# Float64 weights to float32: a two-byte shift of the load, one copy and one shift-and-OR in place of five operations

## Chip, cores and metric

The kernel runs on one core of one Trainium2 chip. The metric is device microseconds of one execution. A NeuronCore has TensorE (PE; its weight loads are listed as PEld), VectorE (DVE), ScalarE (ACT), GpSimd (POOL) and SyncE (SP), which here issues nearly all DMAs, in program order. Sixteen DMA engines serve the core.

## The reference

Three layers follow each other. Four batches with eight heads of causal attention over 576 tokens (head size 64) with a decay term, then a feed-forward layer with a leaky ReLU over 2304 tokens, then a second layer with a SoLU, a layer norm and an output product:

```python
scores = scale * q @ k.T + (cum[:, None] - cum[None, :])   # causal, softmax
x = softmax(scores) @ v                                    # (2304, 512)
h = x @ w_in                                               # w_in (512, 2048), float64
x = np.maximum(0.01 * h, h) @ w_out                        # w_out (2048, 512), float64
h = x @ w_in2                                              # (512, 1024), float64
solu = h * softmax(h)
out = ((solu - mean) / sqrt(var + 1e-6) * g_ln) @ w_out2   # (1024, 512), float64
```

The four weight matrices arrive as float64. [...]

## The kernel before

**Weights.** The weights are cut into 48 chunks of 128 x 512 values (512 KB each as float64): 16 of `w_in` (tiles `wi`, `wib`), 16 of `w_out` (`wo`, `wob`), 8 each of the second layer's matrices (again in `wi` and `wo`). Function `weight` handles a chunk. A DMA brings it into a staging tile (`wst`, three of them, for 17 chunks; later `raw` or `raw2`, two of them, which attention's `kq` loads and layer 2 use as well). ACT writes the absolute value of the upper words into one of two work tiles `wk` (L793). DVE clamps it (L794), shifts it by three bits and masks it (L795), puts the sign bit in (L797) and the upper bits of the lower words (L799). From `wk` a copy to the first half of the weight tile follows (L425 on ACT, L428 on DVE, L432 on POOL), rounded to the format that TensorE takes, and a subtraction (L440, or L436 with a scale) writes the rest to the second half. The staging tile is free after L799, the work tile after the subtraction.

**Order.** A planner (`Plan.run`) goes through all operations before the program is written. Each has a duration by a formula, a priority and the buffers that it needs; the planner hands each engine its next operation, and picks the engine where several are allowed (`flex`, `copy_f`, `sub_f`). What it decides is a fixed program order for each engine; at run time each instruction waits for its inputs in that order.

**Stages.** Sixteen pairs of heads (`pair`) go through attention: score products into `ps_s`, the row maximum (L692, L711), the exponential (L642), a high and a low float16 part of the probabilities `hl` (L425, L436), a transposing DMA `pt<-hl` (L468), and products with V into `ps_v`. Batch 0 (four pairs) is handled together with the first 18 weight chunks. When all `wst` tiles and other early tiles are done with, `main` puts the `x` and `g` tiles in their place, and the first feed-forward blocks (`ffn_a`, nine blocks of 256 tokens, with the first nine `wi` and `wo` chunks) run interleaved with the attention of batches 1 to 3; the block that begins inside batch 1 needs all four pairs of that batch. Then the other 30 chunks are turned, and `ffn_b` and `layer2` follow to the end.

Of the kernel before, what the change touches and what calls it, by code (L numbers as in the profile page):

```python
# [8 lines left out]
F32R = mybir.dt.float32r  # L9
F16 = mybir.dt.float16  # L10
I32 = mybir.dt.int32
BF16 = mybir.dt.bfloat16
AF = mybir.ActivationFunctionType
ALU = mybir.AluOpType
# [50 lines left out]
NEG = -8.0e9  # L65
LNS = 1024.0

F64_LO = 2.0 ** -15
F64_HI = 122876.0
PS = 2.0 ** -15  # L70


# [256 lines left out]
def dve(n):  # L329
    return 1.042 * n + 70  # L330


def dve2(n):
    return 0.521 * n + 70
# [22 lines left out]
def body(tc, kqa, kq, vt, f, one, wa, w2i, w2o, gln, out):  # L357
# [44 lines left out]

    early = ExitStack()
    ep = early.enter_context(tc.tile_pool(name="early", bufs=1, side="right"))
    P.tag("wst", tiles(ep, "wst", NWST, [128, 1024], I32))
    qa = ep.tile([128, 2, KD, 512], F32, name="qa")
    P.tag("qa", [qa])
    P.tag("qb", tiles(ep, "qb", NQB, [128, 2, KB], F32))
# [65 lines left out]
    def setup():  # L474
        nc.gpsimd.memset(qa[64:66, 0], 1.0)
        nc.vector.memset(qa[64:66, 1], 1.0)
        nc.vector.memset(mask, 0.0)
        one_at = P.tags["sd"].free[-1][:, 0:128]
        nc.vector.memset(one_at, 0.0)
        nc.gpsimd.affine_select(  # L480
            one_at, one_at, pattern=[[-1, 128]], compare_op=ALU.not_equal, fill=1.0, base=0, channel_multiplier=1)
        nc.vector.tensor_copy(ident, one_at)
        nc.vector.memset(mask4, 0.0)
        nc.gpsimd.affine_select(
            mask[:, 384:512], mask[:, 384:512], pattern=[[-1, 128]], compare_op=ALU.is_ge,
            fill=NEG, base=0, channel_multiplier=1)
        for o in (0, 64):
            nc.gpsimd.affine_select(
                mask4[o:o + 64, 512:576], mask4[o:o + 64, 512:576], pattern=[[-1, 64]],
                compare_op=ALU.is_ge, fill=NEG, base=0, channel_multiplier=1)  # L490
        nc.gpsimd.memset(halfm, -0.5)
        nc.vector.memset(zcol, 0.0)

    def row(h, p):
# [292 lines left out]

    def weight(src, dst, prio, scale=None, lead=None):
        s, k = P.buf(stage[0]), P.buf("wk")
        load(s, lambda: s.t[:, 0:1024].bitcast(I32), lambda: src.bitcast(I32), 524288, prio - LDW if lead is None else lead)  # L790
        word = lambda j: s.t[:, 0:1024].bitcast(I32).rearrange("p (n t) -> p n t", t=2)[:, :, j]
        kf = lambda: k.t.bitcast(F32)
        P.op(ACT, act(512), lambda: nc.scalar.activation(kf(), word(1).bitcast(F32), AF.Abs), prio, w=[k], r=[s])  # L793
        P.op(DVE, dve2(512), lambda: nc.vector.tensor_scalar(kf(), kf(), F64_LO, F64_HI, op0=ALU.max, op1=ALU.min), prio, rw=[k])  # L794
        P.op(DVE, dve2(512), lambda: nc.vector.tensor_scalar(  # L795
            k.t, k.t, 3, 0x3FFFFFF8, op0=ALU.logical_shift_left, op1=ALU.bitwise_and), prio, rw=[k])
        P.op(DVE, dve(512), lambda: nc.vector.scalar_tensor_tensor(  # L797
            k.t, word(1), -0x40000000, k.t, op0=ALU.bitwise_and, op1=ALU.bitwise_or), prio, rw=[k], r=[s])
        P.op(DVE, dve(512), lambda: nc.vector.scalar_tensor_tensor(  # L799
            k.t, word(0), 29, k.t, op0=ALU.logical_shift_right, op1=ALU.bitwise_or), prio, rw=[k], r=[s])  # L800
        copy_f(lambda: dst.t[:, 0], kf, 512, prio, scale=scale, w=[(dst, 0)], r=[k])
        sub_f(lambda: dst.t[:, 1], kf, lambda: dst.t[:, 0].bitcast(F32), 512, prio, scale=scale, w=[(dst, 1)],
              r=[k, (dst, 0)])

    WI, WO, W2I, W2O = {}, {}, {}, {}
    stage = ["wst"]
# [18 lines left out]
    def hidden(c, xb, n, pst, gt, prio, eprio):  # L825
# [11 lines left out]

        P.op(PE, 12 * mmr(n), pe, prio, w=[ps, (g, "slot")], r=xb + [w])
        h = lambda: ps.t[:, 0:n]
        P.op(ACT, act(n, 0, True), lambda: nc.scalar.activation(g.t[:, 0, 0:n], h(), AF.Prelu, alpha=0.01), eprio, w=[(g, 0)], r=[ps])  # L840
        P.op(ACT, act(n, 0, True), lambda: nc.scalar.activation(h(), h(), AF.Prelu, alpha=0.01), eprio, rw=[ps])  # L841
        P.op(DVE, dve(n) + 60, lambda: nc.vector.tensor_tensor(  # L842
            g.t[:, 1, 0:n], h(), g.t[:, 0, 0:n].bitcast(F32), op=ALU.subtract), eprio, w=[(g, 1)], r=[ps, (g, 0)])
        return g
# [31 lines left out]
    def ffn_a(blk, prio):  # L876
# [4 lines left out]
        for d in range(KD):  # L881
            ps, yo = P.buf("ps_f"), P.buf("yo")
            for q in range(2):
                cs = range(FA // 2 * q, FA if q else FA // 2)

                def pe(cs=cs, d=d, ps=ps):
                    for c in cs:
# [1 line left out]

                P.op(PE, 3 * len(cs) * mmr(TB), pe, prio + EPD + d, r=[gs[c] for c in cs] + [WO[c] for c in cs],  # L890
                     **({"w": [ps]} if q == 0 else {"rw": [ps]}))
            copy_f(lambda yo=yo: yo.t, lambda ps=ps: ps.t[:, 0:TB], TB, eprio + EPD + d, engs=(ACT, DVE), psum=True, w=[yo], r=[ps])
            YPD[blk].append(move(lambda d=d: yp_d[blk][:, d], lambda yo=yo: yo.t, 128 * TB * 4, prio - 3000, r=[yo]))

    def ffn_b(tb, prio):
# [19 lines left out]
        for d in range(KD):  # L915
            y32, y = P.buf("yo"), P.buf("y2")
            yw = yps[d // 2]
            P.op(DVE, dve(TB), lambda d=d, y32=y32, yw=yw: nc.vector.tensor_tensor(
                y32.t, at[d](), yw.t[:, d % 2], op=ALU.add), eprio + 20, w=[y32], r=[py[d], yw])
            copy_f(lambda y=y: y.t[:, 0], lambda y32=y32: y32.t, TB, eprio + 20, w=[(y, 0)], r=[y32])  # L920
            sub_f(lambda y=y: y.t[:, 1], lambda y32=y32: y32.t, lambda y=y: y.t[:, 0].bitcast(F32), TB, eprio + 20,
                  w=[(y, 1)], r=[y32, (y, 0)])
# [66 lines left out]
    def layer2_out(tt, ln, oprio, eprio, deps=()):  # L989
# [8 lines left out]
                mm(po.t, ll, wh, False, c == NC2 - 1)  # L998

        P.op(PE, 24 * mmr(512), pe2, oprio, w=[po], r=list(ln.values()) + list(W2O.values()), deps=deps)  # L1000
        P.op(ACT, act(512, 0, True), lambda: nc.scalar.activation(ot.t, po.t, CP, scale=1.0 / LNS), eprio, w=[ot], r=[po])
        move(lambda: out[128 * tt:128 * tt + 128, :], lambda: ot.t, 262144, -4000, r=[ot])

    def flat(l):
# [125 lines left out]
```

## Time and profile before

| | |
|---|---|
| median of 3 runs | 875.1 us (873.83 to 875.33) |
| profiled execution | 875.05 us, span 873.3 us |
| PE busy | 791.8 us, 91% of the span |
| DVE busy | 581.2 us, 67% |
| ACT busy | 477.8 us, 55% |
| POOL busy | 343.1 us, 39% |
| mean granted clock of TensorE | 0.986 of full speed |

The shares of busy time are means over stages that differ: attention with the first weights (to about 118 us), attention with feed-forward blocks (to about 380 us), the other weights (to about 520 us), and feed-forward and layer 2 alone.

### The profile page before, as it was taken

Reading aid. Unit: us, or ns where it says so; the run is one execution under the profiler, and the core shown is the slowest. Engines: PE = TensorE matmul, PEld = TensorE weight load, DVE = VectorE, ACT = ScalarE, POOL = GpSimd, SP = SyncE. Lnnn points to the kernel's source line nnn. Section 1 sums busy time; section 2 is a strip of 40 time slices with the busy share of each in tenths; the row PEclk is TensorE's granted clock in tenths of the full one; section 3 lists DMA queues with packets and bytes.
Section 4 is the critical chain, followed back from the end, with each engine's and each line's share of the span. In section 5 each row is a group of like instructions: output and inputs, shape, how many; then the busy total and the mean of one; then the engine's idle time right before and its main releaser. Section 6 shows DMA issues by size and latency. Waiting matters only on the chain.

```text
span 873.3 us, 15789 instructions
## 1 busy us (share of the span) xinstructions
PE 791.8 (91%) x5648; PEld 706.2 (81%) x5648; DVE 581.2 (67%) x1405; ACT 477.8 (55%) x1221; POOL 343.1 (39%) x394
## 2 busy tenths in 40 slices
PE   2647799996799999999999999999999999999997
PEld 2323379995689998999999988899988888988985
DVE  6799987888887888858868985424542345234551
ACT  3765778896888988765535543323423243323421
POOL 4465376654674564026212325221422232213321
PEclk9999999998699999999999999999999999999999
DMA  7899589978998895946544423321413041313113
GB/s 217 181 243 232 137 184 191 211 190 184 216 176 202 168 233 134 216 109 187 182 145 134 137 93 85 61 50 48 109 37 69 29 109 38 84 10 77 25 37 96
DMA packets 181960, 114.97 MB, mean 132 GB/s; under 512 B 147030, under 2 KB 163054, under 8 KB 181850
## 3 DMA queue, kind: packets, MB, share of 16 engines
q1 hardware_dynamic: 181882, 113.97, 54.7%
q8 instruction: 44, 0.72, 0.3%
q14 instruction: 34, 0.28, 0.1%
HBM read 64.32 MB, written 15.16 MB: 91 GB/s over the span
## 4 chain that ended last, share of the span: by engine, by line
PE 48%; DVE 4%; DMA 3%; ACT 2%; issue 1%; POOL 0%; SPq 0%; ACTq 0%; DVEq 0%
PE ps_f L471 29%; PE ph L471 11%; PE py L471 7%; DMA raw<-wa 1%; DMA tr<-hl 1%; DVE wk L799 1%; DMA raw<-w2o 1%; DVE g L842 1%; PE ps_v L471 0%; DVE wk L795 0%; PE ps_s L471 0%; DVE x L440 0%; ACT wk L793 0%; DVE wk L794 0%; DVE raw L953 0%
## 5 line engine op out<-in xcount | busy, mean ns | idle before, releaser
L471 PE MATMUL ps_f<-x,wi 128*128 128x256 f32 x972 | 129.2, 287 | 1.2 <-DVE g L842 1.2
L471 PE MATMUL ps_f<-g,wo 128*128 128x256 f32 x972 | 125.4, 283 | 2.0 <-DVE g L842 2.0
L471 PEld LDWEIGHTS ps_f<-x,wi 128*128 128x128 f32 x972 | 122.9, 192 | 2.5 <-DVE g L842 2.0
L471 PEld LDWEIGHTS ps_f<-g,wo 128*128 128x128 f32 x972 | 119.8, 188 | 2.8 <-DVE g L842 2.4
L471 PE MATMUL ps_f<-x,wib 128*128 128x256 f32 x756 | 99.1, 281 | 3.6 <-DVE g L842 1.9
L471 PE MATMUL ph<-wi,g 128*128 128x512 f32 x408 | 98.3, 396 | 0.0
L471 PEld LDWEIGHTS ps_f<-x,wib 128*128 128x128 f32 x756 | 93.1, 188 | 5.1 <-DVE g L842 3.4
L840 ACT ACTIVATE g<-ps_f 128x256 fp32r<-128x256 f32 x144 | 55.3, 384 | 73.9 <-PE ps_f L471 71.9
L642 ACT ACTIVATE ps_s<-ps_s,st 128x512 f32<-128x512 f32 (+4 forms) x160 | 79.1, 494 | 23.6 <-DVE st L692 13.4
L436 DVE SCALAR_TENSOR_TENSOR hl<-ps_s,st,hl 128x512 f16<-128x512 f32 (+4 forms) x160 | 82.0, 538 | 15.0 <-ACT hl L425 13.6
L471 PEld LDWEIGHTS ph<-wi,g 128*128 128x128 f32 x408 | 76.0, 188 | 17.6
L471 PE MATMUL ps_s<-kq 128*128 128x512 f32 (+9 forms) x304 | 72.7, 362 | 13.8 <-DVE hl L436 11.7
L471 PEld LDWEIGHTS <-VT 128*128 128x128 f16 x928 | 55.9, 109 | 35.7 <-issue 16.4
L440 POOL TENSOR_TENSOR kq<-raw,kq 64x576 fp32r<-64x576 f32 (+2 forms) x51 | 77.1, 1513 | 19.2 <-PE ps_f L471 6.3
L425 ACT ACTIVATE hl<-ps_s,st 128x512 f16<-128x512 f32 (+4 forms) x149 | 74.2, 536 | 18.7 <-DVE st L660 11.3
L471 PE MATMUL ps_f<-wo,x 128*128 128x512 f32 x348 | 84.0, 397 | 0.0
L842 DVE TENSOR_TENSOR g<-ps_f,g 128x256 fp32r<-128x256 f32 x144 | 60.2, 419 | 34.0 <-ACT ps_f L841 33.5
L471 PE MATMUL ps_v<-pt,VT 128*128 128x128 f16 (+1 forms) x928 | 64.3, 231 | 17.0 <-DMA pt<-hl 7.2
L471 PEld LDWEIGHTS ps_f<-wo,x 128*128 128x128 f32 x348 | 64.7, 188 | 15.3 <-ACT x L425 0.5
L471 PE MATMUL py<-g,wob 128*128 128x256 f32 x567 | 76.8, 280 | 0.1
L471 PEld LDWEIGHTS py<-g,wob 128*128 128x128 f32 x567 | 72.4, 188 | 2.2 <-issue 0.3
L471 PEld LDWEIGHTS ps_s<-kq 128*128 128x128 f32 (+1 forms) x304 | 53.4, 209 | 23.0 <-DVE hl L436 16.1
(147 smaller groups left out, 1288.1 us busy)
## 6 DMA issues: line engine op xcount, KB each, us to landing
raw<-kq SPq DMA_DIRECT2D x24, 608.0 KB
wst<-wa SPq DMA_DIRECT2D x17, 512.0 KB
raw<-wa SPq DMA_DIRECT2D x15, 512.0 KB
xw<-xs_d SPq DMA_DIRECT2D x24, 256.0 KB
yp_d<-yo SPq DMA_DIRECT2D x36, 128.0 KB
yw<-yp_d SPq DMA_DIRECT2D x18, 256.0 KB
out<-ot SPq DMA_DIRECT2D x18, 256.0 KB
vr<-vt SPq DMA_DIRECT2D x13, 320.0 KB
```

Of the source, the lines that this page charges most:

```text
L425: nc.scalar.activation(o, i, CP, scale=1.0 if scale is None else scale)
L436: nc.vector.scalar_tensor_tensor(o, a, scale, b, op0=ALU.mult, op1=ALU.subtract)
L440: (nc.vector if eng == DVE else nc.gpsimd).tensor_tensor(o, a, b, op=ALU.subtract)
L471: nc.tensor.matmul(o, lhsT=l, rhs=r, start=start, stop=stop)
L642: P.op(ACT, act(W, 1, True) + 93, lambda view=view, j=j, k=k: nc.scalar.activation(view(), view(), AF.Exp, bias=sts.t[:, j:j + 1], scale=- ...
L799: P.op(DVE, dve(512), lambda: nc.vector.scalar_tensor_tensor(k.t, word(0), 29, k.t, op0=ALU.logical_shift_right, op1=ALU.bitwise_or), prio ...
L840: P.op(ACT, act(n, 0, True), lambda: nc.scalar.activation(g.t[:, 0, 0:n], h(), AF.Prelu, alpha=0.01), eprio, w=[(g, 0)], r=[ps])
L842: P.op(DVE, dve(n) + 60, lambda: nc.vector.tensor_tensor(g.t[:, 1, 0:n], h(), g.t[:, 0, 0:n].bitcast(F32), op=ALU.subtract), eprio, w=[(g, ...
```

## The change

The DMA now writes a chunk two bytes further into its staging tile, which is 8 bytes longer. The upper 16 bits of each float64 then lie where they read as a bfloat16, and the 32 bits below them lie on a word boundary. A copy on ACT or POOL with a factor of 0.5 turns the bfloat16 into a float16, written to the upper half of each word of `wk`; this moves the exponent over, and the weight comes out scaled by 2^-8. One DVE operation shifts the lower word right by 13 bits and ORs `wk` in, in place in the staging tile. The copy and the subtraction read the staging tile, every second word, so that it is free only after the subtraction; `wk` is free after the OR. The factor 256 is put back where results are read anyhow: as a scale of the leaky ReLU, of the `yo` copy, of the sum in `ffn_b`, and of the output copy. `wk` is cleared once at the start, by two fills on POOL.

```diff
-    P.tag("wst", tiles(ep, "wst", NWST, [128, 1024], I32))
+    P.tag("wst", tiles(ep, "wst", NWST, [128, 1026], I32))
...
+        for k in P.tags["wk"].free:
+            nc.gpsimd.memset(k, 0)
...
     def weight(src, dst, prio, scale=None, lead=None):
         s, k = P.buf(stage[0]), P.buf("wk")
-        load(s, lambda: s.t[:, 0:1024].bitcast(I32), lambda: src.bitcast(I32), 524288, prio - LDW if lead is None else lead)
-        word = lambda j: s.t[:, 0:1024].bitcast(I32).rearrange("p (n t) -> p n t", t=2)[:, :, j]
-        kf = lambda: k.t.bitcast(F32)
-        P.op(ACT, act(512), lambda: nc.scalar.activation(kf(), word(1).bitcast(F32), AF.Abs), prio, w=[k], r=[s])
-        P.op(DVE, dve2(512), lambda: nc.vector.tensor_scalar(kf(), kf(), F64_LO, F64_HI, op0=ALU.max, op1=ALU.min), prio, rw=[k])
-        P.op(DVE, dve2(512), lambda: nc.vector.tensor_scalar(
-            k.t, k.t, 3, 0x3FFFFFF8, op0=ALU.logical_shift_left, op1=ALU.bitwise_and), prio, rw=[k])
+        half = lambda n, t: s.t[:, 0:n].bitcast(t)
+        load(s, lambda: half(1025, I16)[:, 1:2049], lambda: src.bitcast(I16), 524288, prio - LDW if lead is None else lead)
+        top = lambda: half(1026, BF16).rearrange("p (n t) -> p n t", t=4)[:, 1:513, 0]
+        low = lambda t=I32: half(1024, t).rearrange("p (n t) -> p n t", t=2)[:, :, 1]
+        kf = lambda: low(F32)
+        up = lambda: k.t.bitcast(F16).rearrange("p (n t) -> p n t", t=2)[:, :, 1]
+        copy_f(up, top, 512, prio, engs=T_ENGS, scale=lambda: 0.5, w=[k], r=[s])
         P.op(DVE, dve(512), lambda: nc.vector.scalar_tensor_tensor(
-            k.t, word(1), -0x40000000, k.t, op0=ALU.bitwise_and, op1=ALU.bitwise_or), prio, rw=[k], r=[s])
-        P.op(DVE, dve(512), lambda: nc.vector.scalar_tensor_tensor(
-            k.t, word(0), 29, k.t, op0=ALU.logical_shift_right, op1=ALU.bitwise_or), prio, rw=[k], r=[s])
-        copy_f(lambda: dst.t[:, 0], kf, 512, prio, scale=scale, w=[(dst, 0)], r=[k])
+            low(), low(), 13, k.t, op0=ALU.logical_shift_right, op1=ALU.bitwise_or), prio, rw=[s], r=[k])
+        copy_f(lambda: dst.t[:, 0], kf, 512, prio, scale=scale, w=[(dst, 0)], r=[s])
         sub_f(lambda: dst.t[:, 1], kf, lambda: dst.t[:, 0].bitcast(F32), 512, prio, scale=scale, w=[(dst, 1)],
-              r=[k, (dst, 0)])
+              r=[s, (dst, 0)])
...
-        P.op(ACT, act(512, 0, True), lambda: nc.scalar.activation(ot.t, po.t, CP, scale=1.0 / LNS), eprio, w=[ot], r=[po])
+        P.op(ACT, act(512, 0, True), lambda: nc.scalar.activation(ot.t, po.t, CP, scale=WSC / LNS), eprio, w=[ot], r=[po])
```

The planner orders everything anew with the new operations. DVE's program has 1241 rows where it had 1379; of its 192 operations on the way from float64 to `wk`, 48 are left. Of the 48 new copies 36 stand on ACT and 12 on POOL. Of the subtractions POOL has 24 where it had 30, DVE 24 where it had 18. Three places show what stands where.

DVE while batch 0's attention is handled, before the change: rows of the third and fourth chunk (`wk_83` and `wk_84` are the work tiles, `wst_150` and `wst_152` staging tiles) between rows of softmax (L436, L660, L692).

```order
L692 ISA st_124 128x1
L660 RECIPROCAL st_123<-st_123 128x2
L799 SCALAR_TENSOR_TENSOR wk_83<-wst_152,wk_83 128x512
L794 TENSOR_SCALAR wk_84<-wk_84 128x512
L660 RECIPROCAL st_124<-st_124 128x2
L436 SCALAR_TENSOR_TENSOR hl_126<-ps_s_166,st_123,hl_126 128x128
```

The same place with the change; L439, L665 and L697 are the old L436, L660 and L692, and L802 is the operation with the shift and the OR.

```order
L665 RECIPROCAL st_123<-st_123 128x2
L802 SCALAR_TENSOR_TENSOR wst_150<-wst_150,wk_84 128x512
L665 RECIPROCAL st_124<-st_124 128x2
L697 ISA ps_s_165,st_125<-ps_s_165,mask 128x128
L697 ISA st_125 128x1
L697 ISA ps_s_165,st_125<-ps_s_165,mask 128x256
L697 ISA st_125 128x1
L802 SCALAR_TENSOR_TENSOR wst_151<-wst_151,wk_83 128x512
```

One row for each chunk is left, written to the staging tile instead of `wk`.

SP's queue at the first transposes of batch 0 (`pt_129<-hl_126`), before the change: one weight load, a load of keys and queries (`qb`), and then the transpose.

```order
L462 DMA dr_d<-wo_73 12x2x64
L462 DMA wst_151<-wa 128x1024
L462 DMA qb_154<-kq 64x2x960
L468 DMA_TRANSPOSE pt_129<-hl_126 128x6x128
L462 DMA vre_156<-vt 128x640
```

The same place with the change.

```order
L465 DMA dr_d<-wo_73 12x2x64
L465 DMA wst_150<-wa 128x2048
L465 DMA wst_151<-wa 128x2048
L465 DMA wst_152<-wa 128x2048
L471 DMA_TRANSPOSE pt_129<-hl_126 128x6x128
```

Three weight loads now stand ahead of that transpose, each of which waits for the tile's earlier chunk to be subtracted; the `qb` load has moved ahead, to the place of a weight load.

PE at the end of the second feed-forward block, before the change: the last products with `wo`, and behind them a run of 18 or 20 products with V.

```order
L471 MATMUL ps_f_157<-g_865,wo_80 128x256 x3
L471 MATMUL ps_f_157<-g_866,wo_72 128x256 x3
L471 MATMUL ps_f_157<-g_867,wo_73 128x256 x3
L471 LDWEIGHTS VT_108
L471 MATMUL ps_v_167<-pt_131,VT_108 128x128
```

The same place with the change.

```order
L474 MATMUL ps_f_157<-g_827,wo_72 128x256 x3
L474 MATMUL ps_f_157<-g_828,wo_73 128x256 x3
L474 MATMUL ps_s_165<-kq_0_141 128x512
L474 MATMUL ps_s_165<-kq_1_142 128x512
L474 MATMUL ps_s_164<-kq_0_141 128x128
```

One run of 20 products with V has moved ahead of these rows: from here to the first product of the third block there are 96 of them where there were 116, and 48 score products in both. Ahead of the very first feed-forward product there are 172 products with V where there were 154, and 52 rows of score products in both. From the second half of the program on, PE's rows are the same but for two places where groups have changed order.

## Rows read from the trace of the kernel before

**Rows 1.** Stretches: PE, PEld, DVE, ACT, POOL busy us, granted clock, DMA share, GB/s.

```profile
0.00:40.00 40.00, 17.28 (x55) 11.34 (x55) 29.07 (x91) 21.17 (x65) 19.79 (x28) 1.00 0.83 208
40.00:118.00 78.00, 51.51 (x197) 28.94 (x197) 76.81 (x172) 50.30 (x116) 41.62 (x41) 1.00 0.81 200
118.00:200.00 82.00, 81.29 (x762) 78.34 (x763) 66.30 (x225) 72.73 (x209) 51.19 (x45) 1.00 0.88 190
200.00:240.00 40.00, 25.97 (x177) 22.47 (x177) 32.94 (x101) 30.88 (x82) 20.14 (x23) 0.71 0.87 206
240.00:380.00 140.00, 135.39 (x1275) 128.57 (x1274) 115.09 (x351) 117.74 (x339) 61.88 (x60) 1.00 0.85 182
380.00:420.00 40.00, 37.23 (x316) 36.55 (x315) 30.49 (x46) 21.64 (x54) 23.21 (x24) 1.00 0.54 166
420.00:520.00 100.00, 96.58 (x775) 94.28 (x774) 81.05 (x146) 47.42 (x114) 23.77 (x26) 1.00 0.45 140
520.00:840.00 320.00, 319.29 (x1989) 284.85 (x1988) 137.43 (x263) 108.06 (x235) 94.49 (x139) 1.00 0.26 59
840.00:873.30 33.30, 27.29 (x115) 20.88 (x113) 11.98 (x18) 7.92 (x13) 6.99 (x12) 0.98 0.26 64
```

**Rows 2.** What PE waited for, 0 to 120 us: total, times, longest.

```profile
PE ps_s L471 <- DVE hl L436: 19.7, 11, 5.6
PE ps_s L471 <- DMA qa<-sd: 14.4, 1, 14.4
```

**Rows 3.** DVE on the weight tiles `wk` alone, two stretches.

```profile
0.00:40.00 40.00, 10.96 (x14) 1.00 0.83 208
40.00:118.00 78.00, 46.11 (x58) 1.00 0.81 200
```

**Rows 4.** Staging tile `wst`: duration ns min/median/max, first and last start us.

```profile
L462 SPq DMA_DIRECT2D wst<-wa x17: 328/357/1703, 2.0 to 93.2; - x17
L793 ACT ACTIVATE wk<-wst x17: 644/663/707, 6.3 to 100.3; 128x512 f32<-128x512 f32 x17
L799 DVE SCALAR_TENSOR_TENSOR wk<-wst,wk x17: 664/679/1635, 11.1 to 105.5; 128x512 int32<-128x512 int32 x17
```

**Rows 5.** DVE's group L799, 40 to 118 us: busy us, mean ns.

```profile
L799 DVE SCALAR_TENSOR_TENSOR wk<-wst,wk 128x512 int32<-128x512 int32 x14 | 11.5, 823 | 0.0
```

**Rows 6.** POOL's groups on early weights, whole span: busy us, mean ns.

```profile
L440 POOL TENSOR_TENSOR wi<-wk,wi 128x512 fp32r<-128x512 f32 x12 | 16.9, 1410 | 25.6 <-ACT wi L425 25.5
...
L432 POOL TENSOR_SCALAR wi<-wk 128x512 fp32r<-128x512 f32 x4 | 2.7, 683 | 18.5 <-PE ps_f L471 14.1 <-DVE wk L799 4.3
```

**Rows 7.** Two stretches of 20 us, columns as in the first group.

```profile
0.00:20.00 20.00, 5.46 (x16) 4.23 (x16) 13.89 (x27) 6.78 (x13) 9.82 (x17) 1.00 0.75 226
...
300.00:320.00 20.00, 20.00 (x193) 19.36 (x191) 16.03 (x56) 18.32 (x50) 11.25 (x10) 1.00 0.97 194
```

**Rows 8.** What SP's queue waited for, 0 to 125 us.

```profile
SPq L468 <- DVE hl L436: 24.2, 15, 3.9
SPq L462 <- DVE wk L799: 11.9, 7, 2.9
```

**Rows 9.** What PE waited for, 195 to 245 us.

```profile
PE ps_s L471 <- DVE hl L436: 9.8, 6, 3.7
```

**Rows 10.** What PE waited for, 380 to 520 us.

```profile
PE ps_f L471 <- DVE g L842: 4.7, 5, 1.6
```

**Rows 11.** DVE's groups, 380 to 520 us.

```profile
L797 DVE SCALAR_TENSOR_TENSOR wk<-raw,wk 128x512 int32<-128x512 int32 x28 | 24.5, 876 | 0.7
...
L795 DVE TENSOR_SCALAR wk<-wk 128x512 int32<-128x512 int32 x28 | 14.3, 512 | 0.6
L794 DVE TENSOR_SCALAR wk<-wk 128x512 f32<-128x512 f32 x28 | 14.1, 502 | 7.4 <-ACT wk L793 7.2
```

**Rows 12.** The chain that ended last, start us, us, at the later weights.

```profile
393.56 4.61 DMA raw<-wa
...
413.95 1.26 DVE wk L799
```

More of the change, by code (lines that the diff above doesn't have):

```diff
@@ L11 @@
 I32 = mybir.dt.int32
+I16 = mybir.dt.int16
 BF16 = mybir.dt.bfloat16
@@ L66 @@
 LNS = 1024.0
-F64_LO = 2.0 ** -15
-F64_HI = 122876.0
+WSC = 256.0
+T_ENGS = ("ACT", "POOL")
 PS = 2.0 ** -15
@@ L839, in hidden @@
         h = lambda: ps.t[:, 0:n]
-        P.op(ACT, act(n, 0, True), lambda: nc.scalar.activation(g.t[:, 0, 0:n], h(), AF.Prelu, alpha=0.01), eprio, w=[(g, 0)], r=[ps])
-        P.op(ACT, act(n, 0, True), lambda: nc.scalar.activation(h(), h(), AF.Prelu, alpha=0.01), eprio, rw=[ps])
+        P.op(ACT, act(n, 0, True), lambda: nc.scalar.activation(g.t[:, 0, 0:n], h(), AF.Prelu, scale=WSC, alpha=0.01), eprio, w=[(g, 0)], r=[ps])
+        P.op(ACT, act(n, 0, True), lambda: nc.scalar.activation(h(), h(), AF.Prelu, scale=WSC, alpha=0.01), eprio, rw=[ps])
         P.op(DVE, dve(n) + 60, lambda: nc.vector.tensor_tensor(
@@ L891, in ffn_a @@
                      **({"w": [ps]} if q == 0 else {"rw": [ps]}))
-            copy_f(lambda yo=yo: yo.t, lambda ps=ps: ps.t[:, 0:TB], TB, eprio + EPD + d, engs=(ACT, DVE), psum=True, w=[yo], r=[ps])
+            copy_f(lambda yo=yo: yo.t, lambda ps=ps: ps.t[:, 0:TB], TB, eprio + EPD + d, engs=(ACT, DVE), scale=lambda: WSC * WSC, psum=True, w=[yo], r=[ps])
             YPD[blk].append(move(lambda d=d: yp_d[blk][:, d], lambda yo=yo: yo.t, 128 * TB * 4, prio - 3000, r=[yo]))
@@ L917, in ffn_b @@
             yw = yps[d // 2]
-            P.op(DVE, dve(TB), lambda d=d, y32=y32, yw=yw: nc.vector.tensor_tensor(
-                y32.t, at[d](), yw.t[:, d % 2], op=ALU.add), eprio + 20, w=[y32], r=[py[d], yw])
+            P.op(DVE, dve(TB), lambda d=d, y32=y32, yw=yw: nc.vector.scalar_tensor_tensor(
+                y32.t, at[d](), WSC * WSC, yw.t[:, d % 2], op0=ALU.mult, op1=ALU.add), eprio + 20, w=[y32], r=[py[d], yw])
             copy_f(lambda y=y: y.t[:, 0], lambda y32=y32: y32.t, TB, eprio + 20, w=[(y, 0)], r=[y32])
```

## Prediction, made before the changed kernel ran

> **What bounds the kernel now.** I read the stages first [rows 1]. From 520 to 840 us PE is busy 319.3 of 320 us: nothing done to the weights can shorten that stretch. PE's idle time lies elsewhere, and by stage it is the length less PE's busy time: 22.7 us before 40 us, 26.5 us from 40 to 118 us, 0.7 to 200 us, 14.0 from 200 to 240 us, 4.6 to 380 us, 2.8 and 3.4 to 520 us, 0.7 to 840 us, 6.0 in the last 33 us. Together that is 81.4 us, and 873.3 less PE's 791.8 us is 81.5: nothing is missing.
>
> So the first 118 us hold 49 of the 81 us. Who is late there? PE's longest single wait is for the decay rows that a DMA writes (14.4 us, at the very start), and the largest by total is for `hl` of DVE, 19.7 us in 11 waits [rows 2]. From 40 to 118 us DVE is busy 76.8 of 78 us, ACT 50.3, POOL 41.6, PE 51.5 [rows 1]: DVE is the bound of this stretch. What fills it? The weights: 46.1 of the 76.8 us are operations on `wk` [rows 3].
>
> The second clear gap is 200 to 240 us. DVE is busy 32.9 of 40 us there with no weight work, PE waits for softmax (9.8 us in 6 waits for `hl`) [rows 1, 9], and the granted clock is 0.71, so between the levels of 1.2 and 2.4 GHz, after PE had run at full clock in the stage before and then sat idle in pieces.
>
> **What is removed from DVE.** Up to 118 us the work on `wk` is 10.96 + 46.11 = 57.1 us in 72 operations, that is 18 chunks with four each [rows 3]. One of four is left. It has the form of L799 (two tensors, 512 words, a shift and an OR), whose mean there is 0.82 us [rows 5], between 0.66 and 1.64 us [rows 4]; the ends belong to a free and a disturbed engine, and I take the mean: 18 x 0.82 = 14.8 us stay. Its operands have a step of two words; L799 has one such operand, so that I see no reason for another duration. 57.1 - 14.8 = 42.3 us of DVE go in the first 118 us, some 35 of them between 40 and 118 us (46.1 less 14 x 0.82 = 34.6). From 380 to 520 us three groups go, 24.5 + 14.3 + 14.1 = 52.9 us [rows 11].
>
> **What is added.** The new copy takes the place of L793. On ACT I take L793's own 0.66 us [rows 4], on POOL the 0.68 us of its plain copy of as many values [rows 6]; the bounds are half of that, since the written words are half as long, and the 1.41 us of POOL's two-tensor operation [rows 6]. ACT loses 12 of 48 of them and POOL gains 12. Six subtractions go from POOL to DVE. None of this makes an engine the bound: up to 118 us ACT is busy 71.5 us and POOL 61.4 us of 118 [rows 1]. The two fills of `wk` stand on POOL while PE waits out its 14.4 us for the DMA [rows 2], and are hidden; uncovered, by POOL's copy, they would cost about 1.4 us. The scales by 256 sit in operations that ran before anyway, at the same size: nothing.
>
> **What the first 118 us gain.** If DVE alone counted, the stretch from 40 to 118 us would shrink by 35 us. It doesn't, since the next resource is close: the DMA engines are busy 0.81 of it, 63.2 us [rows 1]. The highest share that a stretch reaches is 0.97 [rows 7]. At 0.95 the same transfers need 63.2 / 0.95 = 66.5 us, and the gain is 11.5 us; at 0.97 it is 12.8. ACT, at the 72.7 of 82 us that it reaches in the next stage, would need 50.3 / 0.887 = 57 us, a gain of 21. So DMA is the bound, and I take **11.5 us** here. In the first 40 us DMA is at 0.83 and DVE busy 29 us [rows 1]; four chunks less 14 operations save 7.7 us of DVE, but the start stands on the 14.4 us wait. Bounds 0 and 3 us, I take 1.
>
> One part works against it. A staging tile was free after L799, and is now free after the subtraction, on POOL mostly (1.41 us) behind a copy (0.63 to 0.68 us) [rows 6]. Three DVE operations of the old chain (3.17 us a chunk for four, by 57.1 / 18) go, so that the hold stays about as long: 3.17 - 0.82 = 2.35 us less, some 2.1 us more. SP's queue is where a late release hurts: it is in order, it waits 11.9 us for L799 and 24.2 us for `hl` [rows 8], and three weight loads now stand ahead of the first transpose, with the transposes and `qb` loads behind them, and PE's score products behind those. As DVE is idle a third of the time then, I price this at nothing; if POOL's subtraction comes late, one such wait costs up to the 2.9 us that the longest wait for L799 took [rows 8].
>
> **The gap at 200 us** has no weight work in it. The order moves one run of 20 products with V ahead of the gap; the 48 score products, on whose softmax PE waits, are the same. I take **1 us**, bounds 0 and 4 (14 us of idle time by the share 20 of 116, and the clock's part).
>
> **The later weights.** From 380 to 520 us PE waits 6.2 us in all, 4.7 of it for DVE's part of the leaky ReLU, which stands behind weight operations [rows 1, 10]. With 53 us of DVE gone most of this goes. But the chain there passes through loads into the two staging tiles (4.61 us) as well as through DVE (1.26 us) [rows 12], and the hold of these tiles doesn't shrink. I take **3 us**, bounds 0 and 6.
>
> **The sum.** 11.5 + 1 + 1 + 3 = 16.5 us. The profiled execution took 875.05 us with a span of 873.3, and the median is 875.1, so that both can be the base: 875.1 - 16.5 = **858.5 us**.
>
> **The load, two bytes on.** No row shows a transfer that starts two bytes past a word. A load is 0.524 MB. At full share the rate is 226 / 0.75 = 301 GB/s in the first 20 us [rows 7] and 200 / 0.81 = 247 GB/s from 40 to 118 us [rows 1], which gives 1.7 to 2.1 us of all engines for a load; I use 1.9. With a factor f on it the 14 chunks of the stretch need (63.2 + 26.6 (f - 1)) / 0.95 us: 72 at f = 1.2 (gain 6), 78.6 at 1.5 (no gain). From below, f = 1. I take 1, because source and run length (4096 bytes a row) stay, and let 1.2 to 1.5 set the upper end. The Trainium skill (DMA: Bandwidth & Descriptors, How a descriptor splits into AXI transactions) says that a run that doesn't begin on a 256-byte boundary takes one more transaction; by that 17 in place of 16, an estimate of 6% or f = 1.06, and the sum would be some 1.6 us less gain, 860 us. The page speaks of reads, and no run here shows it.
>
> **Rivals.**
> - *DMA is no bound, its share is elastic.* Then ACT is next: 21 + 3 + 1 + 3 = 28 us, **847 us**. For it: 0.97 is reached while PE is busy 20 of 20 us [rows 7], so a full DMA need not hold anyone up. Against it: the transposes stand in the same queue as the loads. Chance 0.14.
> - *The staging tiles swallow it.* Each handoff between four engines adds a wait in order, SP's queue passes it on to the transposes, and the first stage gains 0 to 4 us: **868 to 874 us**. For it: rows 8. Chance 0.12.
> - *The gap takes it.* Feed-forward begins 12 us earlier, runs out of work earlier, and waits longer for batch 1, whose softmax has no weights in it and so gains nothing: the gap grows by what the start saved, **870 us**. Against it: batch 1's first score products stand in the same places, so its softmax begins earlier too. Chance 0.06.
> - *Slower: the shifted load takes twice as long.* The stretch needs (63.2 + 26.6) / 0.95 = 94.5 us, 16.5 more than now; the first 40 us, with 33.2 us of DMA and four chunks, 3 more; the later weights, at 28 loads into two tiles, 0 to 27 us, I take 8: **903 us**. It decides from f = 1.55, where the other 4.5 us are used up too. Against it: the same bytes, in rows of 4096. Chance 0.08.
>
> **Chances and range.** My forecast 0.60, the rivals 0.40 as above. A measurement of this kernel can tell about 0.2% (1.75 us) from no change. Faster: 0.60 + 0.14, most of the second rival and half of the third, 0.86; slower: the last, and a part of the third, 0.09; within 0.2%: 0.05. My forecast's own range is 852 to 865 us (early gain 7 to 14, the rest 1 to 9). To leave out no more than 2 in 10 it has to take in most of the first rival and of the second and f = 1.4: 846 to 871 us.
>
> **What would show it.** Right: the first feed-forward product near 106 us instead of 118; a DMA share of 0.93 or more from 30 to 106 us with DVE below 0.7; DVE's busy time near 485 us (581.2 less 101 for three of four operations, and about 5 for the subtractions); PE's busy time unchanged at about 790; the gap still there, some 12 us earlier. The loads of 0.524 MB land as fast as before. Wrong: loads that take 1.5 times as long; SP waiting for the subtraction ahead of the transposes, with DMA share below 0.85; a gap of more than 45 us; a chain through the later loads that makes PE wait more than 6 us from the end of attention to 145 us later.

## The result and the profile after

The changed kernel takes **853.8 us** (median of 4, 849.3 to 854.8) where the kernel before, beside it, takes 875.2 (4 executions, 873.8 to 875.7): a ratio of 0.975, with a 95% interval of 0.971 to 0.978. That is 21.4 us less; 16.5 were forecast, and the range held the time. The profiled execution is the longest of the four, 854.78 us with a span of 852.9, and is compared with the profiled one of before (span 873.3): 20.4 us less.

The head of the page, busy time by engine, then DVE, granted clock and DMA share in the span's 40 slices:

```profile
PE 787.6 (92%) x5648; PEld 707.1 (83%) x5648; DVE 495.8 (58%) x1269; ACT 477.6 (56%) x1208; POOL 338.6 (40%) x402
...
DVE  4787688787778768735544756334442444243641
...
PEclk9999989996799999999999999999999999999999
DMA  7899878899968997646555514231314131312113
```

DVE has lost 85 us of busy time and PE 4. PE's idle time is 852.9 - 787.6 = 65.3 us, where it was 81.5. So 16.2 of the 20.4 us are idle time of PE.

To see where, I cut both spans at the same events, not at the same times: first feed-forward product, first product of the third block, last product with V, first product of the later weights' second half (`py`), last `ph`. After the change, columns as in [rows 1]:

```profile
0.00:106.59 106.59, 66.37 (x270) 41.06 (x270) 73.95 (x220) 73.15 (x177) 63.66 (x76) 0.99 0.90 228
106.59:223.95 117.36, 104.21 (x909) 96.36 (x910) 94.52 (x299) 98.51 (x274) 67.25 (x62) 0.91 0.85 188
223.95:373.60 149.65, 145.56 (x1360) 140.98 (x1361) 110.17 (x354) 126.25 (x361) 68.18 (x71) 0.97 0.81 173
373.60:469.10 95.50, 93.80 (x774) 92.82 (x773) 48.00 (x81) 49.41 (x117) 28.91 (x33) 1.00 0.58 183
469.10:818.30 349.20, 348.51 (x2222) 313.54 (x2221) 155.97 (x298) 122.32 (x266) 103.64 (x150) 1.00 0.28 66
```

Beside the same cuts of before (117.96, 237.58, 383.5, 485.0, 838.3 us; length less PE's busy time is idle time; the third and fourth stage are taken together, since PE's order moves work across the cut between them):

| stage | length before, after | PE idle before, after | saved | forecast |
|---|---|---|---|---|
| to the first feed-forward product | 117.96, 106.59 | 49.2, 40.2 | 11.4 | 12.5 |
| to the third block (holds the gap) | 119.62, 117.36 | 14.7, 13.2 | 2.3 | 1 |
| to the first `py` | 247.42, 245.15 | 7.8, 5.8 | 2.3 | 3, with the next |
| to the last `ph` | 353.3, 349.2 | 3.7, 0.7 | 4.1 | |
| tail | 35.0, 34.6 | 6.0, 5.5 | 0.4 | 0 |

**The first stage.** Stretches of it after the change, and the one of before that was not cut this way in [rows 1]; first after, then before:

```profile
0.00:40.00 40.00, 14.81 (x52) 10.72 (x53) 23.45 (x75) 22.12 (x63) 23.40 (x34) 1.00 0.80 210
40.00:100.00 60.00, 47.73 (x191) 26.89 (x190) 45.99 (x126) 45.75 (x101) 36.02 (x35) 1.00 0.96 244
```

```profile
40.00:100.00 60.00, 37.10 (x130) 19.74 (x131) 59.24 (x126) 38.88 (x88) 32.48 (x29) 1.00 0.89 221
```

DVE was busy 59.2 of 60 us and is now busy 46.0. PE gets through 191 instructions there instead of 130. The DMA share is 0.96. What PE waits for, 0 to 110 us:

```profile
PE ps_s L474 <- DMA qa<-sd: 14.7, 1, 14.7
PE ps_s L474 <- DVE hl L439: 6.7, 4, 2.7
PE ps_s L474 <- DMA qb<-df_d: 5.2, 1, 5.2
PE ps_v L474 <- DMA pt<-hl: 4.9, 2, 2.8
PE ps_v L474 <- DVE xr L732: 3.7, 4, 2.7
PE ps_f L474 <- ACT VT L609: 2.9, 3, 1.5
```

The wait for `hl` fell from 19.7 us in 11 waits [rows 2] to 6.7 in 4. The wait at the very start stayed as it was. Waits for transfers are now 10.1 us together: 5.2 for `qb`, which is new, and 4.9 for `pt`, where the kernel before waited 3.3 us in 2 waits. They looked like the bound that I had forecast; the second experiment tests it.

**A chunk.** The staging tile `wst` after the change, and then the work tile's rows for the later weights (duration ns min/median/max, first and last start):

```profile
L465 SPq DMA_DIRECT2D wst<-wa x17: 328/394/728, 1.9 to 77.5; - x17
L802 DVE SCALAR_TENSOR_TENSOR wst<-wst,wk x17: 682/959/1755, 7.5 to 85.3; 128x512 int32<-128x512 int32 x17
L428 ACT ACTIVATE wk<-wst x15: 763/778/788, 6.6 to 84.1; 128x512 f16<-128x512 bf16 x15
...
L428 ACT ACTIVATE wi<-wst x5: 633/660/672, 10.0 to 59.6; 128x512 fp32r<-128x512 f32 x5
...
L435 POOL TENSOR_SCALAR wi<-wst x4: 639/642/649, 20.3 to 75.8; 128x512 fp32r<-128x512 f32 x4
...
L435 POOL TENSOR_SCALAR wk<-wst x2: 767/768/769, 55.2 to 81.5; 128x512 f16<-128x512 bf16 x2
```

```profile
L802 DVE SCALAR_TENSOR_TENSOR raw<-raw,wk x31: 678/694/1762, 76.8 to 493.1; 128x512 int32<-128x512 int32 x31
L428 ACT ACTIVATE wk<-raw x21: 773/792/808, 75.0 to 479.7; 128x512 f16<-128x512 bf16 x21
```

The last early load is issued at 77.5 us instead of 93.2 [rows 4]. SP's queue, 0 to 110 us:

```profile
SPq L471 <- DVE hl L439: 8.6, 7, 2.2
...
SPq L465 <- POOL wi L443: 1.1, 2, 0.7
...
SPq L465 <- DVE wi L443: 1.1, 1, 1.1
...
SPq L465 <- POOL wo L443: 0.8, 1, 0.8
```

It waits 8.6 us for `hl` where it waited 24.2. In place of the 11.9 us for L799 [rows 8] it waits 3.0 us in 4 waits for the subtractions, on POOL and DVE.

### The profile page after: what moved, and what is told of

It is laid out like the page before. It is cut to its first block, busy times and chain, and to the rows that moved or that the text cites. A ratio compares the mean times of both kernels' runs of the same rounds, so it can differ in the third digit from the quotient of the medians.

```text
span 852.9 us, 15613 instructions
## 1 busy us (share of the span) xinstructions
PE 787.6 (92%) x5648; PEld 707.1 (83%) x5648; DVE 495.8 (58%) x1269; ACT 477.6 (56%) x1208; POOL 338.6 (40%) x402
## 4 chain that ended last, share of the span: by engine, by line
PE 66%; ACT 7%; DMA 6%; DVE 5%; issue 3%; POOL 2%; SPq 0%; ACTq 0%; DVEq 0%; POOLq 0%
PE ps_f L474 41%; PE ph L474 11%; PE py L474 8%; PE ps_s L474 4%; PE ps_v L474 3%; DMA pt<-hl 3%; ACT hl L428 1%; ACT ps_s L647 1%; DMA xw<-xs_d 1%; DVE hl L439 1%; DMA tr<-hl 1%; ACT kq L428 1%; DMA raw<-wa 1%; ACT xr L729 1%; ACT g L843 1%
## 5 line engine op out<-in xcount | busy, mean ns | idle before, releaser
L474 PE MATMUL ps_f<-x,wi 128*128 128x256 f32 x972 | 131.4, 290 | 2.1 <-DVE g L845 2.1
L474 PEld LDWEIGHTS ps_f<-x,wi 128*128 128x128 f32 x972 | 124.9, 195 | 3.3 <-DVE g L845 2.9
L439 DVE SCALAR_TENSOR_TENSOR hl<-ps_s,st,hl 128x512 f16<-128x512 f32 (+4 forms) x160 | 82.4, 540 | 18.6 <-ACT hl L428 17.5
L443 POOL TENSOR_TENSOR kq<-raw,kq 64x576 fp32r<-64x576 f32 (+2 forms) x49 | 74.0, 1510 | 36.6 <-ACT kq L428 34.2
L474 PE MATMUL ps_v<-pt,VT 128*128 128x128 f16 (+1 forms) x928 | 63.2, 230 | 18.6 <-DVE xr L732 9.6
L697 DVE CUSTOM_DVE_ANT_0 ps_s<-ps_s,mask 128x128 f32<-128x128 f32 (+3 forms) x128 | 62.3, 497 | 19.3 <-PE ps_s L474 17.1
```

Of the source, the lines that this page charges most:

```text
L439: nc.vector.scalar_tensor_tensor(o, a, scale, b, op0=ALU.mult, op1=ALU.subtract)
L443: (nc.vector if eng == DVE else nc.gpsimd).tensor_tensor(o, a, b, op=ALU.subtract)
L474: nc.tensor.matmul(o, lhsT=l, rhs=r, start=start, stop=stop)
L697: P.op(DVE, dve(W) + 130, lambda i=i, j=j, view=view: nc.vector.tensor_tensor_reduce(view(), view(), mask[:, 384 - 128 * i:512], -0.125, 3 ...
```

## Experiments

Eleven kernels ran, in three groups on one chip each, with the kernel before beside them (876.3, 877.1 and 877.2 us). Ratios are to that kernel, with 95% intervals; the change itself stands at 0.975 [0.971, 0.978]. One run that would help is missing: the kernel before at its own order, with three of its four DVE operations a chunk left out. It would price the work alone, without a new order.

**1. The load on a word boundary.** Program order is that of the changed kernel, row for row.

```diff
-        load(s, lambda: half(1025, I16)[:, 1:2049], ...
-        top = lambda: half(1026, BF16).rearrange("p (n t) -> p n t", t=4)[:, 1:513, 0]
+        load(s, lambda: half(1024, I16)[:, 0:2048], ...
+        top = lambda: half(1024, BF16).rearrange("p (n t) -> p n t", t=4)[:, :, 3]
...
```

> The changed kernel with each weight load at the start of its staging tile instead of two bytes on; the copy and the merge read other halves of the words, so the weights come out wrong, with the same instructions in the same order on every engine. Theory (a load costs the same at either place, f = 1): 853.8 us within 0.4%, DMA share from 40 to 100 us at 0.96 as in the changed kernel. Rival (the shifted load costs 1.2 to 1.5 times as much): at least 5 us faster than the changed kernel, with the first feed-forward product before 102 us instead of 106.6, and a lower DMA share.

Measured: 852.6 us, ratio 0.972 [0.970, 0.975]. The same time as with two bytes more. Its 40 to 100 us:

```profile
40.00:100.00 60.00, 48.08 (x193) 27.20 (x191) 46.33 (x123) 45.42 (x102) 35.60 (x35) 1.00 0.98 242
```

A share of 0.98 at 242 GB/s, against 0.96 at 244: the shifted load costs nothing that can be seen. Time and share are coarse measures here, since the loads don't hold the stage (experiment 2), and with shifted loads at 244 or 245 GB/s the share of this stretch is 0.96 in the change, 0.99 in experiment 11, 1.01 in experiment 5 and 1.02 in experiment 8. The traces' DMA records are finer. Up to 110 us each of the three kernels has 2304 packets of 4096 bytes, all of them rows of weight loads. Their median is 0.159 us before the change, after it and with the aligned load, and their means are 0.205, 0.187 and 0.182 us.

**2. Fourteen of the 17 early loads left out**, all else in the same order, to price the DMA engines.

```diff
+        n_load[0] += 1
+        skip = 3 < n_load[0] <= 17
+        load(..., none=skip)
...
```

With `none` set, no DMA is issued for that place in the order.

> The changed kernel without 14 of the 17 weight loads into the wst tiles: the first three tiles are turned again and again, so most early weights are wrong; every other instruction stands in the same order. Theory (transfers are the bound of the first 106 us now that DVE is relieved): 14 x 1.9 = 26.6 us of all DMA engines go, the next bound is ACT and the chain of softmax, and the first feed-forward product comes 6 to 12 us earlier than 106.6 us; total 842 to 848 us. Rival (a full DMA holds nobody up; the chain of softmax through DVE, ACT and PE is the bound): the first feed-forward product moves by less than 2 us, total within 0.3% of 853.8 us.

Measured: 849.3 us, ratio 0.969 [0.967, 0.971]; the first feed-forward product at 103.2 us, 3.4 earlier. Its 40 to 100 us, and what PE waited for, 0 to 110 us, without the first wait:

```profile
40.00:100.00 60.00, 49.28 (x194) 28.46 (x192) 47.34 (x133) 46.66 (x107) 36.43 (x36) 1.00 0.69 162
```

```profile
PE ps_s L474 <- DVE hl L439: 7.5, 3, 2.7
PE ps_f L474 <- ACT VT L609: 4.3, 2, 3.4
PE ps_v L474 <- POOL VT L443: 4.1, 1, 4.1
PE ps_v L474 <- DMA pt<-hl: 2.6, 1, 2.6
```

Both numbers missed, on either side of 3.4. The DMA share fell from 0.96 to 0.69 and PE gained 1.6 us in this stretch. The 10.1 us of waits for transfers shrank to 2.6, and waits for `VT`, on POOL and ACT, came in their place. One place shows how close the next wait stood. Behind the score product that waited 5.2 us for `qb` comes a product with V. The changed kernel first, then this run:

```profile
62.31 0.85 PE L474 MATMUL ps_v<-pt,VT 128*128 128x128 f16 x6
```

```profile
61.22 0.82 PE L474 MATMUL ps_v<-pt,VT 128*128 128x128 f16 x6 [4.07 <-POOL VT L443]
```

Without the wait for `qb` the same product starts only 1.1 us earlier, because POOL's part of `VT` isn't ready sooner. So these transfers are worth 3.4 us and are not the bound of the stage, in spite of their share.

**3. Three DVE operations a chunk put back, without the planner's knowing**, so that the program order stays that of the changed kernel.

```diff
...
+            for _ in range(2):
+                nc.vector.tensor_scalar(k.t, k.t, 0, -65536, op0=ALU.logical_shift_left, op1=ALU.bitwise_and)
+            nc.vector.scalar_tensor_tensor(k.t, low(), 0, k.t, op0=ALU.bitwise_and, op1=ALU.bitwise_or)
...
```

> The changed kernel with three more DVE operations for each chunk ahead of the shift and OR (two of the form of L794 and L795, one of the form of L797) that leave the values as they are; the planner does not know of them, so every other instruction stands in the same order. Theory (the time came from DVE's work in the first 118 us and at the later weights): the first feed-forward product goes back to 115 to 120 us, total 868 to 880 us. Rival (the time came from the new order that the planner found): total below 862 us, the first feed-forward product before 111 us.

Measured: 914.3 us, ratio 1.043 [1.040, 1.046]. The 21 us are lost again, and 38 us on top. The first feed-forward product comes at 130.9 us. Its 40 to 100 us, and what PE waited for from 131 to 520 us:

```profile
40.00:100.00 60.00, 31.09 (x110) 16.59 (x110) 53.63 (x124) 34.13 (x79) 28.68 (x29) 1.00 0.70 185
```

```profile
PE ps_f L474 <- DVE g L850: 16.8, 11, 4.2
PE ps_s L474 <- DVE hl L439: 9.2, 7, 2.7
```

That DVE's operations carry the gain is right. The size missed, since I expected about the time of before: in an order that was planned for a short DVE part, the same work costs more than in one planned for it (experiment 4). DVE is busy 53.6 of the 60 us here, less than the 59.2 of before, so that this run doesn't tell DVE's busy time from the longer chain of each chunk.

**4. The same three operations, known to the planner.**

```diff
+        for _ in range(2):
+            P.op(DVE, dve2(512), lambda: nc.vector.tensor_scalar(
+                k.t, k.t, 0, -65536, op0=ALU.logical_shift_left, op1=ALU.bitwise_and), prio, rw=[k])
+        P.op(DVE, dve(512), lambda: nc.vector.scalar_tensor_tensor(
+            k.t, low(), 0, k.t, op0=ALU.bitwise_and, op1=ALU.bitwise_or), prio, rw=[k], r=[s])
```

> The changed kernel with the same three DVE operations put back for each chunk, but as operations of their own that the planner knows, so that it orders everything around them. Theory (of the 60 us that they cost unplanned, only the part that DVE's work itself is worth stays, and the rest was an order that fitted other durations): 868 to 882 us, first feed-forward product at 115 to 121 us. Rival (the shifted load's staging tiles, held until the subtraction, make the old chain longer): 890 us or more.

Measured: 883.5 us (9 executions), ratio 1.007 [1.004, 1.010], a little above the theory's range and below the rival's. The first feed-forward product comes at 127.5 us, later than the 115 to 121 expected and 9.5 us later than in the kernel before, although the total is only 6 us longer: that event alone doesn't give the time. With four DVE operations a chunk again the whole gain is gone. The same work in the two orders differs by 3.6% of the time of before, or 31 us.

**5. The early 18 chunks alone changed.**

```diff
+    def weight(*a, **kw):
+        n_w[0] += 1
+        (weight_new if n_w[0] <= 18 else weight_old)(*a, **kw)
```

> The new way for the first 18 chunks only; the later 30 are turned in the old way with five operations, and so are not scaled by 2^-8, which makes the output wrong. Theory (by stage: 11.4 us up to the first feed-forward product and 2.3 us up to the third block come from the early chunks, the other 6 to 7 us from the later ones): 859 to 863 us. Rival (the later weights give nothing, the later gains follow from the earlier start): 853 to 856 us.

Measured: 859.3 us, ratio 0.980 [0.978, 0.982], as expected. The first feed-forward product comes at 107.4 us.

**6. The later 30 chunks alone** (`n_w[0] > 18` in the same place).

> The new way for the last 30 chunks only; the first 18 are turned in the old way with five operations, and so are not scaled by 2^-8, which makes the output wrong. Theory (the early chunks gave 14 to 16 us, the later ones 5 to 6): 868 to 872 us, with the first feed-forward product at 116 to 120 us. Rival (the two parts are not additive, the later gain needs the earlier start): 873 to 877 us.

Measured: 866.2 us, ratio 0.988 [0.985, 0.991], a gain of 10 us, more than expected. From 380 to 520 us, the early part alone first, then the later part alone:

```profile
380.00:520.00 140.00, 134.44 (x1058) 129.81 (x1058) 115.05 (x198) 68.45 (x166) 52.04 (x58) 1.00 0.47 142
```

```profile
380.00:520.00 140.00, 139.84 (x1136) 137.34 (x1136) 75.15 (x132) 69.26 (x162) 39.65 (x48) 1.00 0.52 158
```

PE is idle 5.6 us there with the old late weights and 0.2 us with the new. The two parts give 2.0% and 1.2%, the whole gives 2.5% [2.2, 2.9]: a little less than their sum.

**7. Loads, copies and ORs of 14 early chunks left out**, order unchanged, to see what is left when the conversion is gone.

```diff
+        flex(T_ENGS, ..., lambda e: None if skip else copy_on(e, up(), top(), 0.5), prio, w=[k], r=[s])
+        P.op(DVE, dve(512), lambda: None if skip else nc.vector.scalar_tensor_tensor(
             low(), low(), 13, k.t, op0=ALU.logical_shift_right, op1=ALU.bitwise_or), prio, rw=[s], r=[k])
...
```

> The kernel without 14 early loads, and also without these chunks' copy on ACT or POOL and their shift and OR on DVE; the rounding copies and subtractions stay, on old data, and every other instruction stands in the same order. Theory (what is left of the first 106 us is attention's own chain in its fixed order, with no engine and no transfer as the bound): first feed-forward product at 99 to 103 us against 103.2 without the loads alone, total 844 to 849 us. Rival (DVE and ACT still bound the stretch by the weights): first feed-forward product before 97 us, total below 843 us.

Measured: ratio 0.965 [0.960, 0.970]; the four executions took 841.5, 848.1, 848.9 and 855.1 us, and the profile is of the longest. In it the first feed-forward product comes at 100.8 us, within the forecast of 99 to 103. From 40 to 100 us PE is busy 50.9 us and DVE 39.6. Beyond the loads, 14 copies and 14 ORs are worth 2.4 us at this event. The rounding copies and the subtractions, most of them on POOL, stayed in this run as in all others, so that their part isn't measured.

**8. Four early chunks of `w_out` in place of eight.**

```diff
-WO0 = 8
+WO0 = 4
```

> The changed kernel with only four instead of eight of the early w_out chunks in the wst tiles; the other five come through the raw tiles at a later priority. Theory (loads of the first stretch cost little, as the run without them showed): within 0.5% of 853.8 us, either way. Rival (the early transfers do hold attention up by some 3 us, and moving them on gives this back): 848 to 851 us.

Measured: 862.8 us, ratio 0.984 [0.981, 0.987], 8 us slower than the change, so that both expectations missed. The first feed-forward product stays at 106.6 us: fewer early weights don't bring it forward. The loss comes later. From 370 to 520 us PE waits mostly as follows, where in the changed kernel it waited 1.7 us in 3 waits for `g` from 373 to 520 us:

```profile
PE ps_f L474 <- DVE g L845: 5.0, 4, 3.4
```

**9. The kernel before, with the staging tile held until the subtraction**, to price the hold.

```diff
-        copy_f(lambda: dst.t[:, 0], kf, 512, prio, scale=scale, w=[(dst, 0)], r=[k])
+        copy_f(lambda: dst.t[:, 0], kf, 512, prio, scale=scale, w=[(dst, 0)], r=[k, s])
...
-              r=[k, (dst, 0)])
+              r=[k, s, (dst, 0)])
```

> The kernel before, with its five operations, but each staging tile counted as in use until the subtraction, as in the changed kernel, instead of until L799. Theory (the hold costs what the run with the three planned operations lost beyond the kernel before, so that it is a term of its own): 5 to 9 us slower than the kernel before, 880 to 885 us. Rival (the hold is priced at nothing, as in the prediction, and that run lost by its order): within 0.3% of the kernel before.

Measured: 870.1 us, ratio 0.992 [0.989, 0.995], so 7 us faster than without the hold. Neither theory allowed for that. The planner, which knows of the hold, made another order, in which the first feed-forward product stands at 152.8 us and the gap at 200 us is filled:

```profile
40.00:100.00 60.00, 46.44 (x188) 26.93 (x187) 56.39 (x148) 42.73 (x104) 30.79 (x28) 1.00 0.91 217
100.00:160.00 60.00, 40.38 (x243) 33.31 (x244) 53.93 (x153) 47.75 (x119) 37.78 (x38) 0.89 0.75 191
...
200.00:240.00 40.00, 38.22 (x355) 36.67 (x353) 31.24 (x97) 34.75 (x99) 21.03 (x24) 1.00 0.89 206
```

PE's idle time moves from the gap at 200 us [rows 1, 9] to the stretch from 100 to 160 us, and less of it is left: from 40 to 240 us PE is busy 164.8 us where it was 158.8. The run tells nothing of the hold by itself; it shows what an order is worth. It shows as well that a first feed-forward product 35 us later can go with a shorter total.

**10. The `qb` loads given a priority 60 earlier** in the changed kernel, against the 5.2 us wait for `qb`.

```diff
-        load((bq, 0), ..., prio - LD)
-        load((bq, "d"), ..., prio - LD, deps=st["full"])
+        load((bq, 0), ..., prio - LD - 60)
+        load((bq, "d"), ..., prio - LD - 60, deps=st["full"])
```

> The changed kernel with an earlier priority (by 60) for the qb loads, the keys and queries for which PE waits 5.2 us at 55 us; the planner orders everything anew. Theory (that wait is the one place where the full transfer queue holds PE up): the wait is gone, first feed-forward product 2 to 5 us earlier, total 847 to 853 us. Rival (another wait takes its place, as in the run with few loads, or the new order costs more): 854 us or more.

Measured: 860.2 us, ratio 0.981 [0.979, 0.983], 5 us slower than the change by the ratios. Waits of PE to 115 us:

```profile
PE ps_s L474 <- DMA qa<-sd: 13.8, 1, 13.8
PE ps_f L474 <- ACT VT L609: 10.8, 3, 5.0
PE ps_s L474 <- DVE hl L439: 9.9, 5, 3.8
```

The wait for `qb` is gone. The wait for `VT` grew from 2.9 to 10.8 us in its place, and the first feed-forward product came 4 us later, at 110.6 us. But this run has another order on every engine: the load of `vre`, from which `VT` is made, starts at 62.3 us where it started at 50.7. So it shows what this order costs, and not what would have been waited for next in the old one.

**11. Weight loads given a priority 4 earlier** in the changed kernel (`LDW` from 52.07 to 56.07), which changes the planner's order alone.

> The changed kernel with the lead of the weight loads' priority at 56.07 instead of 52.07: the same operations, in another order. It measures what order alone is worth. Theory (orders that the planner finds for the same operations differ by less than 1%): 846 to 862 us. Rival (the order is worth as much as the change itself): more than 866 us.

Measured: 851.5 us, ratio 0.971 [0.968, 0.974]. It can't be told from the change, whose interval is 0.971 to 0.978.

## Why the prediction was right, and where it was not

**DVE bounds the first stage.** Right. With three operations a chunk back, in either order, the gain is gone (experiments 3 and 4). The first feed-forward product came at 106.6 us, with 106 forecast. DVE's busy time is 495.8 us, with 485 forecast, although the work taken out is as forecast: the durations of DVE's groups add up to 644.3 us before and 547.8 after, 96.5 less, and 96 were forecast. Records that overlap count once in the busy time, and their overlap fell by 11 us. The 17 early rows of L802 have a mean of 1.02 us where 0.82 was taken, which is 3.4 us. One sign missed: from 30 to 106 us DVE is busy 58.1 of 76 us, a share of 0.76, where below 0.7 was forecast.

**"So DMA is the bound, and I take 11.5 us here."** The time was right, the step was wrong, and that the two agree is luck. The term measured 11.4 us, with the first 40 us, against 12.5. The share is 0.96 from 40 to 100 us, with 0.95 in the sum. But with 14 loads fewer and a share of 0.69 the event moves by 3.4 us only, where a bound at 0.95 would have given 6 to 12 by the estimate of experiment 2. Nor is 0.97 a ceiling. The changed kernel in stretches of 20 us, columns as in [rows 1]:

```profile
40.00:60.00 20.00, 13.82 (x39) 6.88 (x37) 16.94 (x56) 16.62 (x40) 12.43 (x14) 1.00 1.02 256
60.00:80.00 20.00, 14.11 (x59) 8.03 (x60) 15.43 (x31) 15.07 (x32) 14.14 (x13) 1.00 1.02 269
80.00:100.00 20.00, 19.80 (x94) 11.98 (x94) 13.62 (x40) 14.05 (x31) 9.44 (x9) 1.00 0.85 208
```

A share that goes above 1 isn't a part of a whole that can be used up, so that 63.2 us divided by 0.95 gave no bound.

What holds the stage in its place is shown in part. The start still waits 14.7 us for the decay rows. From there to about 79 us PE's idle time is spread over short waits for different releasers (`hl`, `qb`, `xr`, `VT`, `pt`), and where the `qb` wait of 5.2 us was taken away at an unchanged order (experiment 2), a wait for `VT` left 1.1 us of it as gain. This fits a chain of dependent steps through several engines in a fixed order, which I infer and haven't measured by itself; the rounding copies and subtractions of weights, which no run left out, may be a part of it. From 80 to 100 us PE is busy 19.8 of 20 us, and a last wait of 2.8 us for `pt` stands ahead of the first feed-forward product. I take this to be why the rival with an elastic DMA share, which had ACT as the next bound and 847 us, fell short of its 21 us too.

The Trainium skill (Perfetto Trace Analysis, Identifying the Most-Contended Engine) says that the occupancy of DMA misleads, because there are 16 engines, and that the bytes moved against the core's share of memory bandwidth should be read in its place. By the 358 GB/s of memory bandwidth that the page gives for a core (Engine Utilization) the 244 GB/s from 40 to 100 us are an estimate of 68% at most, since they count every byte that the DMA engines moved: over the whole span the trace has 93 GB/s of memory traffic among 135. The trace agrees with the rule in that experiment 2 found little behind a share of 0.96.

**The gap at 200 us.** 2.3 us in place of 1, within the bounds of 0 and 4. It is still there, some 13 us earlier: from 200 to 240 us the granted clock is 0.66, against 0.71 [rows 1]. The rival in which the gap takes the gain would have made this stage longer by 11 us; it is shorter. One thing is new in the stage, and the prediction had no term for it. Its beginning, after the change:

```profile
100.00:118.00 18.00, 15.24 (x119) 14.22 (x118) 14.75 (x46) 13.77 (x35) 10.93 (x13) 0.81 0.69 138
```

From 106 to 110 us the granted clock is 0.50, the level of 1.2 GHz, after PE had waited the 2.8 us for `pt`; before the change it is 1.00 up to 200 us. The first 12 feed-forward products take 2.91 us there, and 12 of the same form 1.65 us at 116 us, at full clock.

**The later weights.** Mis-sized: 3 us forecast, 4.5 measured. I had counted the 6.2 us of PE's idle time from 380 to 520 us and held back half for the loads into two staging tiles. Of the 6.2 us 1.7 are left. The event cut at the first `py` hides this: 3.0 of the 6.2 us lie between 485 and 520 us, and so in the stage to the last `ph`, whose 4.1 us are these 3.0 and 1.1 us of PE's busy time. The experiments give 4.5 us (the change against experiment 5, by the ratios) to 10 us (experiment 6 against before), with other orders. From the third block to the last `ph` 6.4 us are saved; what is left of them, 1.9 us, is 0.6 us of other idle time and 1.3 us of PE's busy time, the 1.1 among them.

**PE's busy time** is 4.2 us less for as many instructions, 2.4 of it before the first feed-forward product, although 18 more products with V stand there. I had forecast no change, and what makes it is open: the trace of one execution for each doesn't tell.

**The shifted load.** f = 1 was right (experiment 1), and with it falls the one rival that ended on the slower side. The estimate of 6% more from the Trainium skill (DMA: Bandwidth & Descriptors, How a descriptor splits into AXI transactions) would be 1.6 us of DMA time in this stretch. The traces show none of it: 6% more would be 0.169 us for a row's packet, and the median is 0.159 us with the shift and without it. The page speaks of reads, and this change moves where the load writes. One figure beside f was worked out wrongly: by the prediction's own formula f = 1.5 gives 80.5 us for the stretch and not 78.6, and the gain is used up at 1.41. The forecast used f = 1 and didn't depend on it.

**The hold priced at nothing.** Not contradicted: SP waits 3.0 us in 4 waits for subtractions, none longer than 1.1 us, and the rival in which the staging tiles swallow the gain, 868 to 874 us, is out. Experiment 9, meant to price it, changed the order and came out faster, so that a price for the hold alone stays open. Experiment 4, with four DVE operations a chunk and the hold, is 0.7% slower than before; those 6 us are hold, new copy and order together.

**The new copy** takes 0.78 us on ACT and 0.77 on POOL where 0.66 and 0.68 were taken. That is 5 to 6 us over 48 chunks, on engines that are busy 56% and 40%, and no row of PE's waits names it.

**What the prediction had no term for** is the planner's order. Orders of nearly the same work lie 0.8% under the kernel before (experiment 9) and 0.6 to 0.9% over the change (experiments 10 and 8). So the terms of a few microseconds, above all the gap and the later weights, are no finer than that, and the 2.5% of the change are about three times as much. How the 2.5% divide into less work and a new order isn't shown, since no run has the old order with the work taken out.

## What to carry to other kernels

A resource at a share of 0.95 is a candidate for the next bound and no more: see how far the share goes in any stretch, and leave the resource's work out at an unchanged order before its share enters a sum. Where a planner writes the order, a change of durations is two changes, the work and the order, and putting the work back once behind the planner's back and once with its knowledge shows how much the order weighs; here the same work differed by 31 us between the two. A single wait that looks removable is worth taking out only if what would be waited for next is much earlier: here, behind 5.2 us of waiting, it was 1.1 us earlier.

## What the runs showed of the hardware that was not expected

- A transfer in rows of 4096 bytes that starts two bytes past a word in on-chip memory runs as fast as one that starts on it: the median packet takes 0.159 us in both, and the kernels 853.8 us shifted and 852.6 aligned.
- With the DMA engines at a share of 0.96 over 60 us, moving 244 GB/s, leaving out 14 loads of 0.524 MB brought 3.4 us. The share reaches 1.02 in two of its stretches of 20 us, so that it isn't a part of a fixed capacity.
- A copy of 128 x 512 values from bfloat16 to float16, both stepped, takes 0.78 us on ACT and 0.77 on POOL, longer than the copies of as many 32-bit values (0.66 and 0.64 to 0.68 us): shorter values brought no time.
- The shift and OR written in place over the staging tile has a median of 0.96 us on the early weights and 0.69 us on the others, with operands of the same form; in both the longest is 1.76 us. The trace puts this beside POOL's work and not the loads: all 26 of the 48 that no POOL instruction overlaps take 0.68 to 0.70 us, in either stage, and the 15 that take more than 0.75 us all run while POOL does, mostly at a two-tensor operation. The one at 32.6 us takes 1.75 us, of which 1.21 lie beside a subtraction on POOL; less the overlap, eight of the 15 take 0.55 us.
